# A new order of all steps in a fused attention and feed-forward kernel, with the key-value sums in three groups

## The chip, the cores and the metric

The kernel runs on one core of a Trainium2 chip. A core has five engines, each with its own list of instructions: TensorE (PE; its weight loads are listed as PEld), VectorE (DVE), ScalarE (ACT), GpSimd (POOL) and SyncE (SP), which here only issues transfers. Engines wait for each other by semaphores. Matrix products land in PSUM, eight banks, which this kernel uses as four pairs. The metric is the device time of one execution in microseconds (us); the median of several runs counts.

## The reference

For 2048 tokens of width 448 the result is `x + A(xn) + B(xn)` with `xn` the layer norm of `x`. A is linear attention with 16 heads of 28, B a feed-forward block of width 1792:

```
q, k, v = split(xn @ wqkv)
pq, pk  = q @ w_phi, k @ w_phi                      # per head
phi     = concat(softmax(p), softmax(-p))           # for q and for k
kv, z   = sum_s phi_k[s]^T v[s],  sum_s phi_k[s]
A       = ((phi_q @ kv) / (phi_q . z + 1e-6)) @ wo
h       = xn @ w1 + b1
B       = (h * tanh(softplus(h))) @ w2              # Mish
```

## The kernel before

All inputs are loaded once and stay on chip. The 2048 tokens are 16 tiles of 128 (t), or 8 pairs of tiles (u). Every step of the program has a short name, and one string, `ORDER`, lists 341 of these names. The steps are called in that order, each step appends its operations to the lists of the engines that it uses (`Program.op`, line 53), and what an operation reads and writes gives its waits. So `ORDER` fixes the order on every engine at once, and also which pair of PSUM banks a product gets (`take2`, line 380: the pair unused the longest), hence whose eviction it waits for. A step that comes later on an engine never overtakes an earlier one that waits.

The names, by stage:

- Loads on SP's queue: `lx..s` (x), `lkms`, `lvms`, `lkts` (key and value weights), `lqT0`..`3` (query weights, transposed), `l1ms` and `l1ts` (W1, main part and last rows), `l2s` (W2), `los` (Wo).
- Layer norm of pair u: `st` (statistics on DVE, `bn` and an aggregate for each tile; `b`: one of the two tiles on ACT), `rs` (reciprocal deviation, on POOL or ACT), `xn` (normalise, `d` on DVE, `p` on POOL, which needs a small `shift` from DVE first), `xt` (transposed copy xT: `a`, `b` by PE and an eviction, `m` by a DMA transpose on SP's queue).
- Weights: `wtk`, `wmk`, `wmq` fold w_phi into the key and query weights (Wpk, Wpq); `qd` copies a few columns of WqT on DVE before `wmq`; `pw` and `bd` prepare the block-diagonal w_phi on POOL.
- Products of pair u: `k`, `q`, `v`. Each has 14 matmuls of 64 rows ("passes") in three parts, A (6), B (6) and H (2), which `ORDER` places one by one; the part that comes last brings the eviction. That is two exponentials on ACT for k (`exk`, to the tile E) and for q (`exq`, to Eq), one copy for v (its engine is the letter of the last part, `a` ACT or `d` DVE).
- `kn{u}.{s}` (lines 623 to 631): half of pair u's key features is summed and inverted on DVE, then scaled on POOL (L630). `kv{u}` (L649): 32 small matmuls that add pair u to the key-value sums, all in one PSUM pair. `kvz` (line 656): DVE evicts the sums into KVT, SP's queue transposes KVT to KVZ.
- `e{t}`: DMA transpose of tile t's query exponentials to EqT. Eq has three homes (u mod 3), so `exq` of pair u waits for the transposes of pair u - 3.
- `f{q}.{fc}` + A, B or H: first feed-forward product, half q of the tokens, chunk fc of 14; 14 passes of 512 columns; the last part brings the Mish on ACT (L699). Exp and Mish lie in different tables of ACT, so each change between them loads a table.
- `nd{t}` (L722): numerator and denominator of tile t, 16 small matmuls, then seven operations on DVE (L738 to L749), the last of which writes the tile `o`. Two buffers hold `o`, for even and for odd pairs. `ot{u}m`: DMA transpose of o (pair u).
- `wo{u}` + part (L845) and `g{t}` (L828): output product and second feed-forward product, added in one bank for each tile; when all four parts are there, `fin` on DVE (L793) adds x. `sto`, `stt`: stores.
- `zero`, `pi`, `pm`, `pp`, `pv`, `pk`: constants written by POOL: zeros for the warm-up products `z12`, the identity, a mask, padding columns of Eq, ones beside v, and `pk` the zeroing of KVT.

Before the change the eight sums stand in a row in `ORDER` but for one `kn` and some `e` (which PE does not see): `kv3 kn6.0 kv0 e0 kv5 kv1 kn6.1 kv2 kv4 e10 e11 kv7 ep kv6 kvz`. Line 423 is the helper `run` that issues all passes of k, q, v and f; line 512 and 510 the evictions on DVE and ACT.

Of the kernel before, what the change touches and what calls it, by code (L numbers as in the profile page):

```python
# [38 lines left out]
class Program:  # L39
# [13 lines left out]
    def op(self, eng, fn, r=(), w=(), dma=False, tag="", after=()):  # L53
        o = Op()
        o.tag, o.parts = tag, None
        o.eng, o.fn, o.dma, o.needed, o.count, o.sem = eng, fn, dma, False, 0, None
        o.idx = len(self.ops[eng])
        deps = list(after)
        for res in list(r) + list(w):
            if res[0] == "ps":  # L60
                deps += [a for e, a in self.psum.get(res, {}).items() if e != eng]
        for res in r:
            if res[0] != "ps":
                deps += self.writers.get(res, [])
        for res in w:
            if res[0] != "ps":
                deps += [d for d in self.writers.get(res, []) if d.dma or dma or d.eng != eng]
                deps += [d for d in self.readers.get(res, []) if d.dma or dma or d.eng != eng]
        for res in r:
            if res[0] == "ps":  # L70
                self.psum.setdefault(res, {})[eng] = o
            else:
                self.readers.setdefault(res, []).append(o)
        for res in w:
            if res[0] == "ps":
                self.psum.setdefault(res, {})[eng] = o
            else:
                self.writers[res] = [o]
                self.readers[res] = []
        o.deps = deps  # L80
        self.ops[eng].append(o)
        self.order = getattr(self, "order", [])
        self.order.append(o)
        return o

    def dma(self, eng, fn, r=(), w=(), tag=""):
        return self.op(eng, fn, r, w, dma=True, tag=tag)
# [57 lines left out]


ORDER = """
table pw lx2s lba zero lx3s lkms pp lps st2b st3b pi pm rs2p lkts z12 rs3a lx1s b1 bd xn2d wtk0b xn3d xt2b lvms wtk1b
lx4s wmk0b st1 lqT2 xt3a v2Ad wmk1a v2Ha lqT0 st4 rs1a v3Ba k2H v2Bd lqT1 lqT3 rs4p qd lx0s xn1d k2A lx6s v3Ha v3Aa
wmq0d wmq1a xn4d k2B k3A k3H xt1m q3B k3B st5 xt4m q3A st0 k1A l1ts pk q1H k1H rs5p q3H q1A k1B v1Hd xn5p rs0p st6  # L150
rs6p st7 xt5m e7 xn0d v1Ad xt0m q1B q2A q2H v1Bd k4B pv xn6d rs7p kn3.1 kn1.1 q2B xn7d k4A k4H e3 v5Bd kn4.0 k5A xt6m
k5H v5Ad k5B v0Ba e6 k0A k0H v0Aa v0Ha k0B kn1.0 v6Bd xt7m l1ms v5Hd q6B v6Ad q6H kn0.1 e4 q6A v7Ba k7B v7Hd v6Ha k7H
k7A k6H kn5.0 k6A v4Bd v7Aa kn2.0 kn0.0 v4Hd e2 l2s v4Ad k6B q4H kn7.1 q4A kn2.1 f1.2B q4B kn5.1 f0.1B f0.0A e9 f0.0H
f0.1A f1.3B f0.1H kn7.0 f1.3H f1.3A f0.0B f0.2B f1.2H e12 f1.2A e13 q7H f0.2A f0.2H q0A q0H f1.1A q0B e5 q7A q5A e8
kn4.1 q5H kn3.0 q7B q5B f1.1H f0.10H f0.10A f1.1B kv3 kn6.0 kv0 e0 kv5 kv1 kn6.1 kv2 kv4 e10 e11 kv7 ep kv6 kvz f1.7B
f0.10B f1.7A f1.7H f1.10A f1.10H f0.3A e1 f1.11H f1.10B f0.3H f1.13H f0.3B f1.11A f1.13B e14 nd2 f1.12B f1.11B f1.13A
f0.9H f1.12A f1.12H nd1 f0.9A f0.8B f0.9B f0.8A nd3 ot1m f0.12A f0.13H f0.8H f0.12B f0.13B f0.12H f1.5B nd6 f1.5A
f1.5H los f0.7A f0.13A f0.11B e15 f1.8B f0.11H nd0 f0.11A f1.8A f1.8H f0.7B f1.0B ot0m f0.7H f0.5A f1.0H f0.5H nd7
f1.0A f0.5B f1.6B f1.4H f1.9H f1.6H f1.9B f1.6A nd5 f1.4A ot3m f1.9A f0.4B f1.4B f0.6B nd4 f0.6A f0.4H f0.6H wo3B
f0.4A nd10 wo1A wo3A wo3H ot2m nd11 g6 g7 g2 wo0H ot5m wo1H nd15 wo0A nd13 wo1B wo0B nd12 g0 g1 g11 ot6m g3 wo5B nd14  # L160
nd8 wo5A wob nd9 ot7m sto3 ot4m wo5H g10 g9 g14 g4 sto0 g8 g5 wo6H wo4H wo2B wo4B wo6B wo7B wo2H wo4A wo2A wo7A wo6A
wo7H g13 sto5 g12 sto6 sto1 sto2 g15 sto4 stt14 stt15
"""


# [5 lines left out]
def _kernel(es, nc, A_x, A_wqkv, A_w_phi, A_wo, B_w1, B_b1, B_w2, out):  # L171
    def sb(name, shape, dtype):
        return es.enter_context(nc.sbuf_tensor(name, shape, dtype))
# [33 lines left out]
    epsT = sb("epsT", [P, 3], FP32)  # L207
# [7 lines left out]
    KVT = sb("KVT", [P, G, 2, 2, 64], BF16)  # L215
# [34 lines left out]
    def bank(b, n=1):  # L250
        return PS[:, b * TCW:(b + n) * TCW]
# [10 lines left out]
    def pb(b):  # L262
        return ("ps", b)
# [82 lines left out]

    def p_kvt():
        op("POOL", lambda e: e.memset(KVT[:, :, :, :, :].rearrange("p g s x f -> p (g s x f)").bitcast(mybir.dt.uint32),
                                      0), w=[("KVT", j) for j in range(4)], tag="pk3")

    def eps_rows():
        for i in range(2):
# [36 lines left out]
    def free2(b):  # L389
        held.discard(b)  # L390
        touch(b, b + 1)
# [264 lines left out]
    def kvz():  # L656
        kvb = kv_bank[0]
        for j in range(4):
            lo, hi = 32 * j, 32 * j + DH + 2
            op("DVE", lambda e, j=j, lo=lo, hi=hi: e.tensor_scalar(  # L660
                KVT[lo:hi, :, :, j // 2, (j % 2) * DH:(j % 2 + 1) * DH],
                bank(kvb)[lo:hi, 0:G * KVW].rearrange("p (g s f) -> p g s f", s=2, f=DH), epsT[lo:hi, 2:3], None,
                op0=ALU.add),
               r=[pb(kvb), ("epsT", 2)], w=[("KVT", j)], tag=f"kvz{j}")
        free2(kvb)
        dma("SP", lambda e: e.dma_start_transpose(KVZ[:, :, :], KVT[:, :, :, :, :].rearrange("p g s x f -> p (g s x f)")),
            r=[("KVT", j) for j in range(4)], w=[("KVZ",)], tag="kvT")
# [231 lines left out]
    for q in range(2):  # L899
        for part in "FABH":  # L900
            for fc in range(FC):
                add(f"f{q}.{fc}{part}", ffn1, q, fc, part)
    add("kvz", kvz)
    add("wob", last_weights)
    add("table", table)
# [16 lines left out]
    for n, fn in (("pi", p_ident), ("pm", p_mask), ("pw", p_wbd), ("pv", p_ones), ("pk", p_kvt), ("pp", p_pads), ("zero", p_zero)):  # L922
        add(n, fn)
# [55 lines left out]
```

## Time and profile before

| what | us |
|---|---|
| median of 3 runs (156.78 to 159.19) | 156.9 |
| the profiled execution: time / its span | 158.34 / 156.0 |
| PE busy | 145.4 |
| DVE busy | 104.2 |
| ACT busy | 74.5 |
| POOL busy | 38.7 |
| last matmul of PE ends at | 152.5 |

In the profile a row of a timeline has the start in us from the span's start, the length, engine, line, operation, what is written from what, and the count; in brackets stand the idle time of the engine before it and what ended that. The chain of waits goes back from the last instruction through what released each. PEclk is the clock that PE was granted, 1.00 being full speed.

### The profile page before, as it was taken

The page shows a single profiled execution, that of the slowest core. Times are in us where ns is not written, and L with a number is a line of the kernel's source. Part 1 is how long each engine was busy: PE and PEld are TensorE (multiplying, and loading weights), DVE is VectorE, ACT ScalarE, POOL GpSimd, SP SyncE. Part 2 cuts the span into 40 slices and gives each one's busy share as a digit, 9 for nine tenths or more (in the row PEclk, how much of TensorE's full clock was granted, in tenths as well). Part 3 has the DMA queues.
Part 4 walks back from the last instruction along what each step waited for, and adds up shares of the span by engine and source line. Part 5 has one row for each costly group of instructions (what it writes and reads, how often), then busy time and mean ns, then how long its engine had stood idle before and what let it go on. Part 6 is the DMA issues. An engine that isn't in the chain of part 4 may idle for free.

```text
span 156.0 us, 3862 instructions
## 1 busy us (share of the span) xinstructions
PE 145.4 (93%) x1669; PEld 75.7 (48%) x1669; DVE 104.2 (67%) x230; ACT 74.5 (48%) x90; POOL 38.7 (25%) x53
## 2 busy tenths in 40 slices
PE   6899998699999984999999999999999999999992
PEld 2365454355544452444443445555555555547451
DVE  1699999999999502209985778993995799003511
ACT  4984999569899894557566567300000000000000
POOL 6403285878999930000000000000000000000000
PEclk9999999999999997899999999999999999999999
DMA  4996659989999938460069531613003040600017
GB/s 131 256 253 195 118 132 177 174 168 305 240 303 215 93 71 133 94 113 4 0 38 256 101 39 25 38 25 59 6 0 59 4 118 0 176 0 4 0 38 256
DMA packets 39964, 17.23 MB, mean 110 GB/s; under 512 B 33932, under 2 KB 39180, under 8 KB 39948
## 3 DMA queue, kind: packets, MB, share of 16 engines
q1 hardware_dynamic: 39776, 16.89, 52.1%
q8 instruction: 13, 0.21, 0.5%
q10 hardware_dynamic: 172, 0.10, 0.2%
q14 instruction: 3, 0.02, 0.1%
HBM read 7.02 MB, written 1.84 MB: 57 GB/s over the span
## 4 chain that ended last, share of the span: by engine, by line
PE 75%; DVE 11%; DMA 6%; issue 3%; POOL 2%; ACT 1%; DVEq 0%; POOLq 0%
PE PS L423 34%; PE PS L828 27%; PE PS L845 7%; DMA xnT<-xn 3%; PE PS L364 3%; DVE xn L497 3%; DMA Wkv<-xn 3%; DVE stats L462 3%; PE PS L722 2%; PE PS L649 2%; DVE v_all L512 1%; POOL xn L492 1%; DVE mv L464 1%; DVE Wpq L512 1%; ACT actT L680 1%
## 5 line engine op out<-in xcount | busy, mean ns | idle before, releaser
L423 PE MATMUL PS<-xnT,W 64*128 64x512 bf16 x392 | 46.2, 383 | 0.3 <-DVE v_all L744 0.3
L828 PE MATMUL PS<-W,actT 128*128 128x448 bf16 (+1 forms) x224 | 42.7, 351 | 0.0
L699 ACT ACTIVATE actT<-PS,b1T 128x1024 bf16<-128x1024 f32 x28 | 30.3, 1113 | 15.0 <-PE PS L423 14.9
L828 PEld LDWEIGHTS PS<-W,actT 128*128 128x128 bf16 x224 | 21.6, 98 | 20.1 <-issue 0.6
L423 PEld LDWEIGHTS PS<-xnT,W 64*128 64x128 bf16 x392 | 18.5, 95 | 22.5 <-issue 2.5
L630 POOL TENSOR_TENSOR actT<-actT,rSk 128x896 bf16<-128x896 bf16 x16 | 26.7, 1701 | 4.1 <-DVE rSk L628 4.1
L793 DVE TENSOR_TENSOR x_all<-PS,x_all 128x448 bf16<-128x448 f32 (+1 forms) x16 | 9.2, 613 | 18.1 <-PE PS L845 10.5
L626 DVE TENSOR_REDUCE Sk<-actT 128x32 f32<-128x896 bf16 x16 | 16.6, 1040 | 0.2 <-ACT actT L618 0.2
L423 PE MATMUL PS<-Wkv,xnT 64*128 64x448 bf16 x112 | 13.2, 349 | 1.9 <-DMA xnT<-xn 1.9
L618 ACT ACTIVATE actT<-PS 128x896 bf16<-128x896 f32 x16 | 13.8, 924 | 1.0 <-DVE rSk L628 0.6
L423 PE MATMUL PS<-Wpk,xnT 64*128 64x448 bf16 x112 | 13.3, 350 | 0.2 <-ACT Wpk L510 0.2
L423 PE MATMUL PS<-Wpq,xnT 64*128 64x448 bf16 x112 | 12.8, 349 | 0.0
L738 DVE COPY Sq<-PS 128x16 f32<-128x16 f32 x32 | 4.0, 167 | 12.0 <-PE PS L722 11.9
L749 DVE TENSOR_TENSOR xn<-v_all,rden 128x448 bf16<-128x448 f32 x16 | 10.0, 625 | 2.4 <-DMA Wkv<-xn 1.8
L462 DVE BATCH_NORM_STATS2 stats<-x_all 128x6 f32<-128x448 bf16 x14 | 8.4, 601 | 3.4 <-DMA x_all<-in_A_x_dram 3.4
L746 DVE TENSOR_TENSOR v_all<-v_all 128x464 f32<-128x464 f32 x16 | 10.3, 642 | 0.6
L742 DVE TENSOR_TENSOR v_all<-PS,Sq 128x464 f32<-128x464 f32 x16 | 10.3, 641 | 0.5
L744 DVE TENSOR_TENSOR v_all<-PS,Sq 128x464 f32<-128x464 f32 x16 | 10.1, 630 | 0.0
L423 PEld LDWEIGHTS PS<-Wkv,xnT 64*128 64x128 bf16 x112 | 5.7, 94 | 6.7 <-issue 2.7
L680 ACT ACTIVATE actT<-PS 128x896 bf16<-128x896 f32 x10 | 8.5, 925 | 0.7 <-PE PS L423 0.7
L497 DVE TENSOR_SCALAR xn<-x_all,mv,rstd 128x448 bf16<-128x448 bf16 (+2 forms) x21 | 8.5, 458 | 0.0
L423 PEld LDWEIGHTS PS<-Wpk,xnT 64*128 64x128 bf16 x112 | 5.7, 94 | 5.4 <-ACT Wpk L510 0.6
(83 smaller groups left out, 117.7 us busy)
## 6 DMA issues: line engine op xcount, KB each, us to landing
W<-in_B_w_dram SPq DMA_DIRECT2D x1, 1568.0 KB, 8.6
out_dram<-x_all SPq DMA_DIRECT2D x7, 224.0 KB, 2.2
W<-in_B_w_dram SPq DMA_DIRECT2D x1, 1344.0 KB, 7.0
x_all<-in_A_x_dram SPq DMA_DIRECT2D x4, 224.0 KB, 3.3
x_all<-in_A_x_dram SPq DMA_DIRECT2D x2, 448.0 KB, 4.8
Wkv<-in_A_wqkv_dram SPq DMA_DIRECT2D x2, 336.0 KB, 4.8
Wo<-in_A_wo_dram SPq DMA_DIRECT2D x2, 336.0 KB, 4.4
W<-in_B_w_dram SPq DMA_DIRECT2D x2, 224.0 KB, 3.7
```

The lines of the kernel that those rows point to most:

```text
L423: ins = e.matmul(o, lhs(c, k), rhs(c, k), start=first and n == at[par][0], stop=last and n == at[par][-1])
L462: op("DVE", lambda e, t=t: e.bn_stats(stats[:, t, :], x_all[:, t, :]), r=[("x", t)], w=[("st", t)], tag=f"bn{t}")
L497: op("DVE", lambda e, t=t, lo=lo, hi=hi, at=at: e.tensor_scalar(X[:, at:at + hi - lo], x_all[:, t, lo:hi], mv[:, t, 0:1], rstd[:, t:t + 1] ...
L618: op("ACT", lambda e, s=s: e.activation(E_of(u)[:, s, :, :], two(b, D), ACT.Exp, scale=1.0 if s == 0 else -1.0), r=[pb(b), pb(b + 1)], w=[ ...
L626: op("DVE", lambda e: e.tensor_reduce(Sk[u][:, s, :], Eh(), AX.X, ALU.add), r=[("E", u, s)], w=[("Sk", u, s)], tag=f"Sk{u}.{s}")
L630: op("POOL", lambda e: e.tensor_tensor(Eh(), Eh(), ap_on(rSk[u][:, s, 0:1], [[1, 2 * H], [0, DH]]), ALU.mult), r=[("E", u, s), ("rSk", u, ...
L699: op("ACT", lambda e: e.activation(actT[:, fc, q * 1024:(q + 1) * 1024], bank(b, 2), ACT.Mish, bias=b1T[:, fc:fc + 1]), r=[("b1T",), pb(b) ...
L742: op("DVE", lambda e: e.tensor_tensor(tv(t1[i]), num(0), sx(1), ALU.mult), r=[pb(b), pb(b + 1), ("Sq", i, 1)], w=[("t1", i)], tag=f"ta{t}")
L744: op("DVE", lambda e: e.tensor_tensor(tv(t2), num(1), sx(0), ALU.mult), r=[pb(b), pb(b + 1), ("Sq", i, 0)], w=[("t2",)], tag=f"tb{t}")
L746: op("DVE", lambda e: e.tensor_tensor(t1[i], t1[i], t2, ALU.add), r=[("t1", i), ("t2",)], w=[("t1", i)], tag=f"tc{t}")
L828: ins = e.matmul(bank(b)[:, 0:width(t)], actT[:, fc, tok(t)], W2[:, fc, 0:width(t)], start=first and fc == 0, stop=last and fc == FC - 1)
L845: ins = e.matmul(bank(b)[:, 0:w], oT_of(u)[lo:hi, cc * P:(cc + 1) * P], Wo[lo:hi, cc, 0:w], start=first and n == at[par][0], stop=last and ...
```

## The change

All 341 steps get a new order. What the products, the evictions and the stores compute is unchanged. Beside the order itself:

- the eight sums stand in three groups, `kv5 kv0 kv2`, then `kv7 kv4 kv6`, then `kv3 kv1`. On PE `q7A q5A f0.13A q5H f0.13B` stand between the first two, `f0.13H f0.6H f0.6A f0.10A f0.6B f0.10B` between the last two;
- the part that ends v2 is `v2Aa`, so ACT evicts it and not DVE;
- `e3 e2` come ahead of `l1ms`; `l2s`, `e15` and `los` come behind `kvz`; `l1ts` ahead of `xt4m`;
- POOL begins with `pv` instead of `pw`, `pw` moves behind `rs2p`, and `pp` moves behind `pk`;
- the zeroing of KVT writes a resource of its own, ("KVT0",), and `kvz` reads it, where the zeroing had written the four resources that `kvz` writes.

```diff
--- before.py
+++ after.py
@@ -145,21 +145,21 @@
 
 
 ORDER = """
-table pw lx2s lba zero lx3s lkms pp lps st2b st3b pi pm rs2p lkts z12 rs3a lx1s b1 bd xn2d wtk0b xn3d xt2b lvms wtk1b
-lx4s wmk0b st1 lqT2 xt3a v2Ad wmk1a v2Ha lqT0 st4 rs1a v3Ba k2H v2Bd lqT1 lqT3 rs4p qd lx0s xn1d k2A lx6s v3Ha v3Aa
-wmq0d wmq1a xn4d k2B k3A k3H xt1m q3B k3B st5 xt4m q3A st0 k1A l1ts pk q1H k1H rs5p q3H q1A k1B v1Hd xn5p rs0p st6
-rs6p st7 xt5m e7 xn0d v1Ad xt0m q1B q2A q2H v1Bd k4B pv xn6d rs7p kn3.1 kn1.1 q2B xn7d k4A k4H e3 v5Bd kn4.0 k5A xt6m
-k5H v5Ad k5B v0Ba e6 k0A k0H v0Aa v0Ha k0B kn1.0 v6Bd xt7m l1ms v5Hd q6B v6Ad q6H kn0.1 e4 q6A v7Ba k7B v7Hd v6Ha k7H
-k7A k6H kn5.0 k6A v4Bd v7Aa kn2.0 kn0.0 v4Hd e2 l2s v4Ad k6B q4H kn7.1 q4A kn2.1 f1.2B q4B kn5.1 f0.1B f0.0A e9 f0.0H
-f0.1A f1.3B f0.1H kn7.0 f1.3H f1.3A f0.0B f0.2B f1.2H e12 f1.2A e13 q7H f0.2A f0.2H q0A q0H f1.1A q0B e5 q7A q5A e8
-kn4.1 q5H kn3.0 q7B q5B f1.1H f0.10H f0.10A f1.1B kv3 kn6.0 kv0 e0 kv5 kv1 kn6.1 kv2 kv4 e10 e11 kv7 ep kv6 kvz f1.7B
-f0.10B f1.7A f1.7H f1.10A f1.10H f0.3A e1 f1.11H f1.10B f0.3H f1.13H f0.3B f1.11A f1.13B e14 nd2 f1.12B f1.11B f1.13A
-f0.9H f1.12A f1.12H nd1 f0.9A f0.8B f0.9B f0.8A nd3 ot1m f0.12A f0.13H f0.8H f0.12B f0.13B f0.12H f1.5B nd6 f1.5A
-f1.5H los f0.7A f0.13A f0.11B e15 f1.8B f0.11H nd0 f0.11A f1.8A f1.8H f0.7B f1.0B ot0m f0.7H f0.5A f1.0H f0.5H nd7
-f1.0A f0.5B f1.6B f1.4H f1.9H f1.6H f1.9B f1.6A nd5 f1.4A ot3m f1.9A f0.4B f1.4B f0.6B nd4 f0.6A f0.4H f0.6H wo3B
-f0.4A nd10 wo1A wo3A wo3H ot2m nd11 g6 g7 g2 wo0H ot5m wo1H nd15 wo0A nd13 wo1B wo0B nd12 g0 g1 g11 ot6m g3 wo5B nd14
-nd8 wo5A wob nd9 ot7m sto3 ot4m wo5H g10 g9 g14 g4 sto0 g8 g5 wo6H wo4H wo2B wo4B wo6B wo7B wo2H wo4A wo2A wo7A wo6A
-wo7H g13 sto5 g12 sto6 sto1 sto2 g15 sto4 stt14 stt15
+pv table lx2s lba zero pm st2b lx3s lkms lps st3b lkts z12 pi b1 rs2p pw rs3a xn2d bd lx1s wtk0b lvms lx4s xn3d xt2b
+wtk1b wmk0b lqT2 xt3a v2Ha wmk1a v2Ba lqT0 st1 v3Ha lqT1 lqT3 rs1a v3Aa v2Aa st4 rs4p pk v3Ba k3H lx0s k3A qd xn1d
+wmq0d wmq1a k2H k3B lx6s pp k2A st5 q3A xn4d k2B q3B rs5p q2A xt1m l1ts q3H k1A q2H xn5p xt4m st0 v1Ad k1H st6 xt5m e7
+rs0p q2B st7 xn0d v1Bd k1B v1Hd rs7p rs6p k4A k4H q1B k4B xn6d q1H q1A v4Ad k5H xn7d v4Hd k5A v4Bd v5Ad kn1.0 xt0m k5B
+v5Bd k0B xt6m v5Hd xt7m v0Ba kn2.1 kn2.0 k0H k0A e3 k6H k6A kn0.0 e2 v6Ba l1ms k6B v0Ha kn0.1 v0Aa v6Aa v6Ha k7H k7A
+q4B e6 k7B v7Aa v7Ha kn7.0 q4H q4A q6A q6H v7Ba e9 q6B kn6.0 f0.2B kn5.1 f0.0A f1.2A f0.2A f0.0H f1.2H kn6.1 e5 f1.3B
+f0.2H f0.0B e12 f1.2B f1.3A kn4.1 f0.3B kn5.0 f1.3H e13 f0.3H f0.1B e4 f0.3A f0.1H f0.1A q7H q0A kn3.1 q0H kn4.0 q5B
+e8 q0B q7B kv5 kn7.1 e0 kv0 kv2 q7A q5A f0.13A q5H f0.13B kv7 kv4 e10 kv6 f0.13H f0.6H f0.6A kn3.0 f0.10A f0.6B kn1.1
+f0.10B kv3 kv1 ep f0.10H f1.7H f1.7A e11 f1.9A kvz f1.7B f0.12B f1.5B f0.12A f1.5H f0.5H f1.9H f0.12H l2s f1.9B f1.5A
+f0.5A f1.1A nd3 f1.1B f0.5B e15 f1.0A f1.1H f1.13B f1.0H f1.13H f1.0B nd2 los f1.13A ot1m f1.8B f0.9H f1.8A f1.8H nd0
+f0.11B f0.9A f0.11A f0.11H f0.7A f0.7H f0.8B nd6 e14 f0.8H f0.9B f0.7B e1 f0.8A f1.12H f1.12A f1.10A nd7 f1.10B f1.4H
+f1.10H f1.12B ot3m f1.4A nd1 f1.6B f1.4B f0.4H f1.6A ot0m f0.4A wo1H f1.6H f0.4B nd4 wo1A wo3A wo1B wo3H nd5 ot2m g1
+g3 g2 f1.11A f1.11H nd11 wo0B f1.11B wo3B wo0A nd13 wo0H nd10 g6 ot5m g0 g7 g11 nd12 wo2A wo5A sto1 ot6m wo5H wo2B
+nd15 nd9 g10 sto0 g5 nd14 ot7m wo2H wo5B nd8 g4 g9 g14 g13 g12 g8 sto3 ot4m wo4H wo4A wo6B wo7B sto2 wo6H wo6A sto5
+wo4B sto4 wo7H wob wo7A g15 stt14 sto6 stt15
 """
 
 
@@ -346,7 +346,7 @@
 
     def p_kvt():
         op("POOL", lambda e: e.memset(KVT[:, :, :, :, :].rearrange("p g s x f -> p (g s x f)").bitcast(mybir.dt.uint32),
-                                      0), w=[("KVT", j) for j in range(4)], tag="pk3")
+                                      0), w=[("KVT0",)], tag="pk3")
 
     def eps_rows():
         for i in range(2):
@@ -661,7 +661,7 @@
                 KVT[lo:hi, :, :, j // 2, (j % 2) * DH:(j % 2 + 1) * DH],
                 bank(kvb)[lo:hi, 0:G * KVW].rearrange("p (g s f) -> p g s f", s=2, f=DH), epsT[lo:hi, 2:3], None,
                 op0=ALU.add),
-               r=[pb(kvb), ("epsT", 2)], w=[("KVT", j)], tag=f"kvz{j}")
+               r=[pb(kvb), ("epsT", 2), ("KVT0",)], w=[("KVT", j)], tag=f"kvz{j}")
         free2(kvb)
         dma("SP", lambda e: e.dma_start_transpose(KVZ[:, :, :], KVT[:, :, :, :, :].rearrange("p g s x f -> p (g s x f)")),
             r=[("KVT", j) for j in range(4)], w=[("KVZ",)], tag="kvT")
```

## The prediction

> **What bounds the kernel now.** I read the page first: share of the engines, the slices, the chain that ended last.
>
> ```profile
> span 156.0 us, 3862 instructions
> PE 145.4 (93%) x1669; PEld 75.7 (48%) x1669; DVE 104.2 (67%) x230; ACT 74.5 (48%) x90; POOL 38.7 (25%) x53
> PEclk9999999999999997899999999999999999999999
> q8 instruction: 13, 0.21, 0.5%
> PE 75%; DVE 11%; DMA 6%; issue 3%; POOL 2%; ACT 1%; DVEq 0%; POOLq 0%
> ```
>
> TensorE (PE) bounds it. The order moves work about but drops no product, so it can win only what PE loses: its gaps, and the time at a low clock. So next I read PE's timeline for every gap behind the start. A matmul's row ends about 0.26 us after the next may start, so I measure a gap from start to start, with the spacing of passes (one 64-row matmul of a product) from stretches without a gap.
>
> ```profile
> 10.70 0.93 PE L423 MATMUL PS<-Wkv,xnT 64*128 64x448 bf16 x8
> 11.84 0.36 PE L423 MATMUL PS<-Wpk,xnT 64*128 64x448 bf16 x2 [0.21 <-ACT Wpk L510]
> ...
> 13.17 0.92 PE L423 MATMUL PS<-Wkv,xnT 64*128 64x448 bf16 x8
> 14.16 0.96 PE L580 MATMUL PS<-Wbd,WqT 112*128 112x112 bf16 x16
> ...
> 24.26 0.92 PE L423 MATMUL PS<-Wpk,xnT 64*128 64x448 bf16 x8
> 25.64 0.74 PE L423 MATMUL PS<-Wkv,xnT 64*128 64x448 bf16 x6 [0.46 <-DMA xnT<-xn]
> ...
> 27.52 0.75 PE L423 MATMUL PS<-Wpk,xnT 64*128 64x448 bf16 x6
> 29.72 0.74 PE L423 MATMUL PS<-Wkv,xnT 64*128 64x448 bf16 x6 [1.45 <-DMA xnT<-xn]
> 30.29 0.94 PE L423 MATMUL PS<-Wpk,xnT 64*128 64x448 bf16 x8
> 31.04 0.75 PE L423 MATMUL PS<-Wkv,xnT 64*128 64x448 bf16 x6
> ...
> 42.47 6.24 PE L423 MATMUL PS<-xnT,W 64*128 64x512 bf16 x56
> 48.55 0.35 PE L423 MATMUL PS<-Wpq,xnT 64*128 64x448 bf16 x2
> ...
> 54.04 1.89 PE L423 MATMUL PS<-xnT,W 64*128 64x512 bf16 x16
> 56.23 2.01 PE L649 MATMUL PS<-actT,v_all 128*30 128x56 bf16 x223 [0.30 <-ACT actT L680]
> 60.85 0.58 PE L649 MATMUL PS<-actT,v_all 128*30 128x56 bf16 x33 [2.62 <-issue]
> ...
> 83.11 2.32 PE L423 MATMUL PS<-xnT,W 64*128 64x512 bf16 x20
> 85.77 2.12 PE L423 MATMUL PS<-xnT,W 64*128 64x512 bf16 x18 [0.33 <-DVE v_all L744]
> ```
>
> Eight passes of 448 columns take 31.04 - 30.29, 0.094 us each; 56 of 512 take 48.55 - 42.47, 0.109 each. The gaps are then: 11.84 - 10.70 - 8 x 0.094 = 0.39; 14.16 - 13.17 - 0.75 = 0.24; 25.64 - 24.26 - 0.75 = 0.63; 29.72 - 27.52 - 0.56 = 1.64; 56.23 - 54.04 - 16 x 0.109 = 0.45; 85.77 - 83.11 - 20 x 0.109 = 0.48. The largest stands in the key-value sums (L649). The windows show it, and what follows it:
>
> ```profile
> 56.20:58.05 1.85, 1.82 (x223) 1.82 (x224) 0.00 (x0) 1.83 (x3) 0.00 (x0) 1.00 0.20 37
> 58.05:60.85 2.80, 0.18 (x22) 0.08 (x11) 0.00 (x0) 2.16 (x2) 0.00 (x0) 0.91 0.65 94
> 60.85:63.74 2.89, 2.89 (x45) 1.32 (x46) 1.79 (x4) 0.00 (x0) 0.00 (x0) 0.50 0.51 96
> 63.74:66.65 2.91, 2.91 (x30) 1.28 (x28) 0.00 (x0) 2.12 (x2) 0.00 (x0) 1.00 0.74 143
> ```
>
> Columns: stretch, its length, busy time of PE, PEld, DVE, ACT, POOL, then PE's clock. 224 weight loads go in 1.85 us, then 2.80 us of nothing, then 2.89 us at half clock, which loses 2.89 x 0.5 = 1.45. Every loss together: 0.63 at the start (two gaps) + 0.63 + 1.64 + 0.45 + 2.80 + 1.45 + 0.48 = 8.1 us.
>
> **What the 2.80 us wait for.** The view names no releaser ("issue"). The last of the eight sums, kv6, needs POOL's last normalisation; that had ended 2 us earlier. What does fall there is a fetch of instructions, the only one in its window:
>
> ```profile
> 36.14 19.92 POOL L630 TENSOR_TENSOR actT<-actT,rSk 128x896 bf16<-128x896 bf16 x12 [0.56 <-DVE rSk L628]
> q8 instruction: 1, 0.02, 5.8%
> ```
>
> POOL's row ends at 56.06. The second row is the window 57.9 to 59.4. The page counts 13 such fetches for 2 x 1669 weight loads and matmuls, one for some 257; PE eats the sums' 512 in about two microseconds, two fetches' worth. I read the gap as PE out of instructions: its 449th of the stretch could start only 60.85 - 56.23 = 4.62 us after the first. (The Trainium skill, Runtime: NRT & Kernel Launch, Instruction fetch mechanics, gives blocks of 256 instructions, with which 257 agrees, but room for 2048 on PE and fetches mostly hidden. By that the gap is no fetch and splitting the sums wins nothing there: first rival below.)
>
> **The change, part by part.**
>
> *Sums in three groups* (kv5 kv0 kv2, kv7 kv4 kv6, kv3 kv1). A sum takes 1.85/7 = 0.26 us. Between the groups stand 14 passes of q7 and q5 with 12 of f0.13: 14 x 0.094 + 12 x 0.109 = 2.62 us; then 28 ffn1 passes, 3.05. Now 448 instructions from the first sum on last 0.79 + 2.62 + 0.79 + 6 passes, 0.65 = 4.85, against the 4.62 that supply needed: no gap. The sums also start 22 passes earlier in PE's list (q7A, q5A, q5H and 8 of f0.10 no longer precede them), so the fetch falls elsewhere; then PE meets the same limit at 448 + 44 = 492 instructions, after 0.79 + 2.62 + 0.79 + 3.05 = 7.25 us. I take 2.80 as gone; at worst 4.62 - 4.20 = 0.4 of it stays, with the limit right behind the second group. Without a gap over 2 us I see no cause for half clock: 1.45 gone. (The Trainium skill, TensorE: Matmul & The Clock Gate, Part 1, lets the clock fall after an idle window of about 3.4 us. The gap was 2.80 and the clock fell; by the rule as stated the 1.45 would not be tied to this gap, and the sum would be 1.45 higher.)
>
> *v2's eviction goes from DVE to ACT.*
>
> ```profile
> 12.91 1.06 DVE L512 CAST v_all<-PS 128x896 bf16<-128x896 f32 x1
> 13.89 0.21 DVE L286 COPY WqT<-WqT 128x256 bf16<-128x256 bf16 x1
> 16.08 3.37 ACT L618 ACTIVATE actT<-PS 128x896 bf16<-128x896 f32 x4
> ```
>
> The copy in WqT (qd) stood behind it, and PE's L580 at 14.16 behind qd (0.24). Without it qd ends near 13.1. The k passes that waited for Wpk (0.39) now stand behind all of v3. So both go: 0.63. ACT takes the 1.06 in time it waited for v3.
>
> *xT5, xT0, xT6, xT7.* DVE runs about 0.9 us ahead from there.
>
> ```profile
> 24.54 5.04 DMA xnT<-xn
> xnT<-xn SPq DMA_TRANSPOSE x6, 3.3
> ```
>
> xT5 is sent earlier (its shift no longer stands behind bn0 and bn1 on DVE) and its user k5H comes behind k4, q1 and v4A: 0.63 gone. xT0 left at 24.54 and took 5.04, against a median 3.3. It leaves 0.9 to 1.6 earlier, so lands between 26.2 and 28.7. k0B, now its first user, stands 12 passes further down than v0B did: 29.72 - 2.90 (gaps gone) + 12 x 0.094 = 27.95. I let 0.5 of the 1.64 stay (bounds 0 and 0.75).
>
> *W1 behind e3 and e2.* e3 waits for q1's exponentials, now the seventh pair on ACT: from 16.08 - 0.63, 14 x 0.84 (row above) gives 27.2; two issues of 1.31 more, and the load leaves at 30.
>
> ```profile
> W<-in_B_w_dram SPq DMA_DIRECT2D x1, 1344.0 KB, 7.0
> 25.90 1.31 SPq L688 DMA_TRANSPOSE EqT<-actT  x1
> ```
>
> It lands near 37. The first ffn1 pass stands 84 ffn1 and 28 q passes ahead of the sums; these start at 56.23 - 3.35 (gaps) - 22 x 0.094 = 50.8, so it stands at 39.0. Covered by 2 us; beyond that each microsecond costs one. W2, Wo and e15 go behind the sums' transpose; W2's first user g1 comes after 90, 25 us later: nothing.
>
> *POOL and DVE before the sums.* First normalisation after v4's eviction (v4B ends 18 passes ahead of k0B, 26.3; + 1.06 + 1.33 = 28.7); 16 x 19.92/12 = 26.6 gives 55.3. kv1 stands at 50.8 + 7.5 = 58.3, kv7 (needs the 14th, 51.9) at 55.0. Covered by 2 to 3.
>
> ```profile
> 46.54 1.03 DVE L626 TENSOR_REDUCE Sk<-actT 128x32 f32<-128x896 bf16 x1
> 47.87 1.03 DVE L626 TENSOR_REDUCE Sk<-actT 128x32 f32<-128x896 bf16 x1
> ```
>
> *Second half.* The 0.48 at 85.77 comes from DVE, which waited 1.84 us to write o until the transpose of its buffer's former content had landed:
>
> ```profile
> 73.13 0.26 DVE L738 COPY Sq<-PS 128x16 f32<-128x16 f32 x2
> ...
> 76.15 0.25 DVE L738 COPY Sq<-PS 128x16 f32<-128x16 f32 x2
> ...
> 83.69 0.63 DVE L749 TENSOR_TENSOR xn<-v_all,rden 128x448 bf16<-128x448 f32 x1 [1.84 <-DMA Wkv<-xn]
> ```
>
> An nd takes DVE 76.15 - 73.13 = 3.0 us; its write of o comes last. Now nd0, of the other buffer, stands between nd2 and nd6, so 3.0 + 2.5 us lie between the send and the write, against 3.3 for a transpose: gone. nd4 right behind nd1 may wait 0.8 so, but no PE step follows close. On PE, nd3, nd2, nd0, nd6, nd7 stand 36, 22, 34 and 34 passes apart (3.9, 2.4, 3.7, 3.7 us), a pace that DVE can follow.
>
> *The KVT tie and the other POOL steps: nothing.* kvz waited for the memset before too; it ends 45 us ahead of its use, and behind kvz nothing new queues. pv takes pw's place ahead of zero at like size; pw hides in POOL's wait for rs2p and Wraw; pp is done before the first q exponential at about 19.
>
> *Hand-offs grown tight.* Counting through the new list, about ten steps have under 0.5 us to spare (f1.3B on q6's exponentials, f0.10A on q5's, wo3A on ot3, nd11 on fin2). I take 0.8 for all, bounds 0 and 2.
>
> Sum: 8.1 - 0.5 - 0.8 = 6.8 us off the profiled span, 156.0 to 149.2. That execution took 158.3 in all, 2.3 around its span; the median of the runs shown is 156.9, and 156.9 - 6.8 = **150.1**.
>
> **Rivals.**
> 1. The gap is not supply (POOL later than its row says, or any cause that follows the sums): 2.80 and 1.45 stay, 150.1 + 4.25 = 154.4. For: no releaser is named, and it stopped exactly at kv6. Against: POOL's row, the fetch. 0.09.
> 2. The early transposes and W1 come no sooner: 0.63, the rest of 1.64 and 1.5 for W1 come back, 150.1 + 3.3 = 153.4. For: xT0's 5.04 shows how such a transfer can stretch. Against: margins above. 0.12.
> 3. Slower: splitting makes PE run dry twice, at both block ends inside the sums. Two gaps of 2.80 with 1.45 each, 150.1 + 8.5 = 158.6. It decides if supply takes over 7.2 us and not 4.62. 0.04; another 0.05 for tight hand-offs adding up to over 10 us, past 160.
>
> **Numbers.** Forecast 0.70, from 148.8 (all 8.1) to 152. With rival 2 the range is 148.8 to 153.4. Two per cent, about what these runs (156.8 to 159.2) can tell, is 3.1: under 153.8 lie the forecast and rival 2, less a little, 0.81; within, rivals 1 and 3, 0.14; slower 0.05.
>
> **What would show it.** Right: no "issue" idle of PE in the sums, clock 1.00 throughout, sums from about 51 to 59, PE busy without a gap over 0.7 to about 145. Wrong: a gap between the groups; PE waiting on xnT, W or POOL's L630 between 25 and 58; DVE's o rows waiting on a transpose while PE's wo steps wait on them.

## The result and the profile after

| | before | after |
|---|---|---|
| median, us (runs) | 158.05 (156.78 to 159.19, 4) | 151.06 (150.73 to 151.37, 4) |
| profiled execution: time / span | 158.34 / 156.0 | 150.73 / 148.7 |
| PE busy | 145.4 | 144.0 |

The ratio is 0.963, with a 95% interval of 0.959 to 0.968: the change takes 3.7% off. The prediction said 150.1 us, and 149.2 for the span.

The median of before depends on which executions it catches. In the 47 further executions of before that ran beside the experiments, 24 show a mean clock of about 0.989 (158.6 us and a span of 156.2 in the mean), and 23 a clock of about 1.00 (157.0 and 154.7). All executions of after show 0.997 to 1.00.

The page of after, from top to chain:

```profile
span 148.7 us, 3864 instructions
PE 144.0 (97%) x1669; PEld 74.2 (50%) x1669; DVE 102.7 (69%) x229; ACT 74.7 (50%) x91; POOL 38.9 (26%) x53
PEclk9999999999999999999999999999999999999999
PE 92%; DMA 3%; DVE 2%; SPq 1%; issue 0%
```

PE's share of the chain went from 75% to 92%, "issue" from 3% to 0%, and the dip in PEclk is gone. The windows over the three groups of sums of after; columns as in the prediction (stretch, length, busy time of PE, PEld, DVE, ACT, POOL, PE's clock, DMA share and rate):

```profile
50.82:51.70 0.88, 0.88 (x99) 0.84 (x98) 0.81 (x5) 0.87 (x3) 0.88 (x2) 1.00 0.00 0
51.70:54.47 2.77, 2.77 (x34) 1.10 (x27) 1.59 (x1) 2.77 (x5) 2.77 (x2) 1.00 0.63 51
54.47:55.35 0.88, 0.88 (x98) 0.84 (x97) 0.00 (x0) 0.88 (x2) 0.88 (x2) 1.00 0.53 11
55.35:58.48 3.13, 3.13 (x39) 1.28 (x30) 0.00 (x0) 3.10 (x4) 1.32 (x2) 1.00 0.66 127
58.48:59.11 0.63, 0.63 (x66) 0.59 (x64) 0.00 (x0) 0.63 (x1) 0.00 (x0) 1.00 2.07 212
```

In every row PE is busy for the whole length, at clock 1.00. PE's waits over the whole span of after are two, both before 7 us:

```profile
PE PS L364 <- POOL mask L327: 1.4, 1, 1.4
PE PS L556 <- DMA Wkv<-in_A_wqkv_dram: 0.4, 1, 0.4
```

How much PE gained is read from its last group of matmuls (L810), in before and in after:

```profile
152.43 0.57 PE L810 MATMUL PS<-W,actT 128*128 128x64 bf16 x14
```

```profile
145.34 0.57 PE L810 MATMUL PS<-W,actT 128*128 128x64 bf16 x14
```

That is 7.09 us of the 7.3 by which the spans differ; the other 0.2 lies in what follows PE.

### The profile page after: what moved, and what is told of

Its sections match the earlier page's. It is cut to its first block, busy times and chain, and to the rows that moved or that the text cites. A ratio compares the mean times of both kernels' runs of the same rounds, so it can differ in the third digit from the quotient of the medians.

```text
span 148.7 us, 3864 instructions
## 1 busy us (share of the span) xinstructions
PE 144.0 (97%) x1669; PEld 74.2 (50%) x1669; DVE 102.7 (69%) x229; ACT 74.7 (50%) x91; POOL 38.9 (26%) x53
## 4 chain that ended last, share of the span: by engine, by line
PE 92%; DMA 3%; DVE 2%; SPq 1%; issue 0%
PE PS L423 50%; PE PS L828 29%; PE PS L845 7%; DMA Wkv<-in_A_wqkv_dram 3%; PE PS L722 3%; PE PS L649 2%; PE PS L580 1%; DVE xn L497 1%; SPq L270 1%; PE PS L556 0%; PE PS L505 0%; DVE x_all L793 0%; DVE Eq L512 0%; DVE x_all L814 0%
## 5 line engine op out<-in xcount | busy, mean ns | idle before, releaser
L423 PE MATMUL PS<-xnT,W 64*128 64x512 bf16 x392 | 44.8, 377 | 0.0
L699 ACT ACTIVATE actT<-PS,b1T 128x1024 bf16<-128x1024 f32 x28 | 29.8, 1112 | 22.1 <-PE PS L423 22.1
L423 PEld LDWEIGHTS PS<-xnT,W 64*128 64x128 bf16 x392 | 17.9, 94 | 21.9 <-PE PS L423 1.9
L423 PEld LDWEIGHTS PS<-Wpq,xnT 64*128 64x128 bf16 x112 | 5.4, 94 | 5.0 <-ACT actT L680 0.2
```

The lines of the kernel that those rows point to most:

```text
L423: ins = e.matmul(o, lhs(c, k), rhs(c, k), start=first and n == at[par][0], stop=last and n == at[par][-1])
L699: op("ACT", lambda e: e.activation(actT[:, fc, q * 1024:(q + 1) * 1024], bank(b, 2), ACT.Mish, bias=b1T[:, fc:fc + 1]), r=[("b1T",), pb(b) ...
```

## The experiments

The first two experiments start from the kernel before, all others from the kernel after, and every edit moves steps in `ORDER` alone; what is computed stays the same. The theory is the prediction's: PE runs out of instructions in the row of sums, and the other gaps go by earlier work on DVE and SP. The rivals are that the stop has another cause, which the order takes away by the way, and that other parts of the new order carry the gain. A diff shows only the stretch of `ORDER` that moves; what stands before and behind it on the line is left out.

| run | median us (executions) | ratio to before, 95% | spans |
|---|---|---|---|
| sums split in before | 156.68 (10) | 0.995, 0.990 to 0.999 | 153.8 to 155.0 |
| the same, first nd later | 156.28 (10) | 0.994, 0.990 to 0.997 | 153.6 to 154.3 |
| sums in one row in after | 155.02 (4) | 0.985, 0.976 to 0.995 | 152.2 to 153.8 |
| row 12 passes later | 154.84 (1) | | 152.8 |
| row without transposes | 156.03 (1) | | 154.0 |
| after again | 151.18 (6) | 0.958, 0.952 to 0.963 | 148.7 to 149.4 |
| W2 early | 152.27 (6) | 0.965, 0.957 to 0.972 | 149.8 to 152.1 |
| v2 on DVE | 152.57 (4) | 0.966, 0.959 to 0.973 | 149.5 to 150.7 |
| xn5 later | 151.72 (1) | | 149.7 |
| b1 later | 151.21 (6) | 0.958, 0.953 to 0.963 | 148.6 to 149.0 |
| lkms second | 151.28 (6) | 0.957, 0.952 to 0.963 | 148.9 to 149.3 |
| both of these | 151.33 (6) | 0.958, 0.954 to 0.963 | 148.8 to 149.1 |

**1. The split alone, in before.** The eight sums become three groups, with passes from right behind them put between:

```diff
-f1.1B kv3 kn6.0 kv0 e0 kv5 kv1 kn6.1 kv2 kv4 e10 e11 kv7 ep kv6 kvz f1.7B
-f0.10B f1.7A f1.7H f1.10A f1.10H f0.3A
+f1.1B kn6.0 kn6.1 kv4 kv3 kv0 e0 f0.10B f1.7B f1.7A kv5 kv1 kv2 e10 e11
+f1.7H f1.10A f1.10H kv7 ep kv6 kvz f0.3A
```

> The order of before with one thing changed: the eight sums in three groups, kv4 kv3 kv0, then 18 ffn1 passes, kv5 kv1 kv2, then 10 ffn1 passes, kv7 kv6. Supply theory (PE runs out of instructions when 448 of them go in under 2 us): no idle over 0.3 us in the sums, clock 1.00 all along, span 156.0 - 2.80 - 1.45 = 151.8 (151.3 to 152.4). Rival (the gap is a wait of the sum kv6 for POOL or another producer): a gap of 2 to 3 us stays in front of kv6's group and the span stays within 1 us of before.

The gap is gone, and the mean clock stayed at 0.997 to 1.00 in all ten executions. Yet the span expected, 151.3 to 152.4, was missed: the spans have a mean of 154.4, only about 0.3 us under those of before without the low clock (154.7). PE's timeline of the split kernel around the sums:

```profile
57.23 0.95 PE L649 MATMUL PS<-actT,v_all 128*30 128x56 bf16 x96 [0.85 <-ACT actT L680]
...
63.29 4.37 PE L423 MATMUL PS<-xnT,W 64*128 64x512 bf16 x36
68.69 0.40 PE L722 MATMUL PS<-KVZ,EqT 56*128 56x60 bf16 x16 [1.03 <-DMA KVZ<-KVT]
```

PE's waits of before list no KVZ at all; here PE waits 1.03 us for it, and 0.85 for ACT ahead of the sums. The wait for KVZ comes of my edit: it took 28 passes from behind the sums, so 36 are left to cover DVE's eviction and the transpose, which need 68.69 - 63.29 = 5.4 us. In before the stretch from the sums' end to nd2 held 64 passes, part of them at half clock, so the slow clock was cover:

```profile
61.36 8.26 PE L423 MATMUL PS<-xnT,W 64*128 64x512 bf16 x64
```

So the 2.80 us of the gap are not all to be had by removing it alone. How much of them other lateness ate (the 0.85 for ACT stands ahead of the sums, where before waited 0.30, and no gap covered that) was not followed to the end.

**2. The first nd later, in the split kernel.** nd2 goes behind two more ffn1 parts:

```diff
-f1.13B e14 nd2 f1.12B f1.11B f1.13A
+f1.13B e14 f1.12B f1.11B nd2 f1.13A
```

> split_in_before with one thing more: 12 ffn1 passes moved from behind the first nd step to ahead of it, so that PE has 1.3 us more work while the sums are evicted and transposed. Theory: the 2.8 us that the split freed came back as waits behind it, 1.3 of them at that nd step, since 28 of the passes that had covered the transpose were used up between the groups. With the cover back, PE's wait for KVZ is under 0.3 and the span 1.0 to 1.3 below split_in_before's (153.8 to 155.0), so 152.6 to 153.9. Rival: the split's gain is lost elsewhere and the span stays.

The wait for KVZ is gone; spans are about 0.4 us shorter than in experiment 1, not the 1.0 to 1.3 expected. Two waits on ACT stand in the view of PE's waits:

```profile
PE PS L649 <- ACT actT L680: 0.5, 1, 0.5
PE PS L423 <- ACT actT L699: 0.4, 1, 0.4
```

The exponentials of k and q, and the Mish behind them, are in time only in the new order. The split in before's order thus gives back the half clock and at most a microsecond more (spans of 154.0 in the mean, against 154.7).

**3. One row again, in after.** The passes between the groups go ahead of the sums:

```diff
-q7B kv5 kn7.1 e0 kv0 kv2 q7A q5A f0.13A q5H f0.13B kv7 kv4 e10 kv6 f0.13H f0.6H f0.6A kn3.0 f0.10A f0.6B kn1.1
-f0.10B kv3 kv1 ep f0.10H f1.7H
+q7B kn7.1 e0 q7A q5A f0.13A q5H f0.13B kn3.0 kn1.1 e10 f0.6A f0.6B kv5 kv0 kv2 kv7 kv4 kv6 kv3 kv1 ep f0.13H
+f0.6H f0.10A f0.10B f0.10H f1.7H
```

> The order of after with one thing undone: the eight sums in one row, kv5 first and kv1 last, in the place between the products that had stood between them. Supply theory: PE stops at the same place of its instruction list as in the kernel before, its 727th weight load; the row begins behind 519, so after 208 loads of the row, inside the seventh sum. Gap 2.5 to 3 us, then about 3 us at half clock; span 148.7 + 4.3 = 153.0 (152.2 to 153.8). Rival (a wait of one sum for its producer): a stop in front of a sum, after 192 or 224 loads, or none.

The gap comes back, in the sums but not at the same sum: here PE stops inside the seventh, where before it stopped at the eighth.

```profile
56.00 2.01 PE L649 MATMUL PS<-actT,v_all 128*30 128x56 bf16 x207
60.06 0.56 PE L649 MATMUL PS<-actT,v_all 128*30 128x56 bf16 x49 [2.05 <-issue]
```

Two executions kept the clock (spans 152.2 and 152.3), two have 0.987 to 0.989 (153.6 and 153.8). Against after's 149.1 the row costs 3.2 us without the low clock and 4.6 with it. Of the 3.2, 2.4 is the row's longer stay (60.55 - 56.00 = 4.55, against 2.1 for eight sums). It also starts 1.2 later than after's first sum and the 38 passes now ahead of it make (50.82 + 14 x 0.094 + 24 x 0.109 = 54.75). Half of that, 0.6, is there from the start (PE's first product passes stand at 10.16, in after at 9.56); most of the rest lies in two gaps of under 0.4 ahead of the row, which were not followed.

**4. The row 12 passes later.** As 3, with `f0.10A f0.10B` ahead of the row too. If the stop hangs on a step or a transfer, it stays at that sum; if it hangs on the number of instructions, it comes 12 matmuls of the sums earlier.

```diff
-e10 f0.6A f0.6B kv5 kv0
+e10 f0.6A f0.6B f0.10A f0.10B kv5 kv0
```

> As row_in_after, with 12 more ffn1 passes ahead of the row. Supply theory: the stop comes 12 loads earlier in the row, after 196 of its loads, again the 727th of the list, with the same gap of 2.5 to 3 us. Rival: the stop stays in front of the same sum as in row_in_after, or goes, since its producers have 1.3 us more.

```profile
57.05 2.08 PE L649 MATMUL PS<-actT,v_all 128*30 128x56 bf16 x195
61.07 0.66 PE L649 MATMUL PS<-actT,v_all 128*30 128x56 bf16 x61 [1.93 <-issue]
```

It moved by 207 - 195 = 12 matmuls. So the stop hangs on no step and no transfer. The windows from zero to a point in the gap count every matmul (first x) and weight load (second x) up to the stop, in before, in 3 and in 4:

```profile
0.00:58.06 58.06, 53.41 (x726) 28.55 (x727) 46.58 (x97) 48.41 (x67) 38.48 (x52) 1.00 0.89 190
```

```profile
0.00:57.90 57.90, 55.62 (x726) 29.74 (x726) 45.27 (x96) 50.99 (x69) 38.58 (x52) 1.00 0.75 163
```

```profile
0.00:59.05 59.05, 56.65 (x726) 30.12 (x726) 45.05 (x96) 51.02 (x69) 38.48 (x52) 1.00 0.75 165
```

Three orders, three points among the sums and three times, and each stops behind the 726th matmul of PE's list. (Experiment 5 does too: x726 up to 58.50.) No semaphore, bank or transfer of the program is common to these places; the count of instructions is.

**5. The row with no transpose beside it.** As 3, with `e10` and `e11` behind `kvz`, to see whether transfers on SP's queue lengthen the gap.

```diff
-kn1.1 e10 f0.6A
+kn1.1 f0.6A
...
-f1.7A e11 f1.9A kvz f1.7B
+f1.7A f1.9A kvz e10 e11 f1.7B
```

> As row_in_after, with the two query transposes e10 and e11 behind the sums' own transpose, so that no transpose is in flight when PE's instructions are fetched. If the fetch is slowed by transposes beside it (its packet took 1.40 us in before against 0.93 in the median), the gap is 0.4 to 1 us shorter than in row_in_after, 1.8 to 2.4 us, and may leave the clock at 1.00. If the gap is the fetch's own latency, it stays within 0.2 us.

The gap, and the DMA view of the window 56 to 60.2 in 40 slices of 0.105 us:

```profile
55.98 1.87 PE L649 MATMUL PS<-actT,v_all 128*30 128x56 bf16 x207
60.19 0.56 PE L649 MATMUL PS<-actT,v_all 128*30 128x56 bf16 x49 [2.35 <-issue]
```

```profile
DMA  0000000000000070000000000000000000000000
q8 instruction: 1, 0.02, 2.0%
```

One instruction fetch, from about 57.5, is all that moves; the gap is 2.35 against 2.05 with transposes. So it isn't contention that makes it long. PE stops at 57.85, after the fetch began, and goes on 2.6 us behind its start. Half of that is the packet itself: 2.0% of 16 engines over 4.2 us are 1.3 us (in before 1.4, with a median of 0.97 over its 13 fetches). What passes in the other 1.3 us the trace doesn't show. Then the clock fell, as it does in about half of before's executions:

```profile
61.09:64.50 3.41, 3.28 (x16) 0.73 (x14) 1.53 (x4) 2.12 (x2) 0.00 (x0) 0.50 0.21 42
```

**6. W2 early.** The load of W2 goes back ahead of the query transposes, the prediction's "nothing":

```diff
-v7Ha v7Ba e9 q6B
+v7Ha v7Ba l2s e9 q6B
...
-f0.12H l2s f1.9B
+f0.12H f1.9B
```

> The order of after with one thing undone: the load of W2 stands ahead of e9 again, as in the kernel before, and not behind the sums' transpose. The prediction put the move at nothing: span within 0.3 of after. Rival: the 1.6 MB lie in front of the query transposes e9 to e8, which land some 6 us later, the exponentials q0 and q7 wait for their home and PE for their banks: 1 to 3 us more.

The median span is 150.25 against 149.1, and the profiled one is 2.2 longer: the expectation's rival came true. PE's timeline, ACT's, SP's, and the DMA issues at 33.5, all of W2 early:

```profile
55.44 0.82 PE L423 MATMUL PS<-xnT,W 64*128 64x512 bf16 x6 [2.46 <-ACT Eq L680]
```

```profile
52.36 1.28 ACT L680 ACT_TABLE_LOAD   x1 [2.86 <-DMA EqT<-Eq]
```

```profile
33.52 1.03 SPq L300 DMA_DIRECT2D W<-in_B_w_dram  x1
39.13 6.34 SPq L688 DMA_TRANSPOSE EqT<-actT  x2
45.51 2.69 SPq L688 DMA_TRANSPOSE EqT<-Eq  x2
48.24 3.80 SPq L688 DMA_TRANSPOSE EqT<-actT  x2
```

```profile
W<-in_B_w_dram SPq DMA_DIRECT2D x1, 1568.0 KB, 12.2
```

W2 takes 12.2 us here (7.9 in after), with W1, sent at 31.61, still in flight beside it until about 38.4, and the last of the transposes is sent by 52.0. In after, SP's timeline has them out by 47.3:

```profile
41.80 2.71 SPq L688 DMA_TRANSPOSE EqT<-Eq  x2
44.56 2.71 SPq L688 DMA_TRANSPOSE EqT<-actT  x2
```

An exponential that reuses a home of Eq, and the table load ahead of it, wait for the transpose, and PE waits for that exponential's bank. The move costs nothing at W2's own user, as predicted; but without it the passes among the sums are late. It is worth 1 to 2 us.

**7. v2 on DVE.** The eviction goes back to DVE:

```diff
-v3Aa v2Aa st4 rs4p
+v3Aa st4 v2Ad rs4p
```

> The order of after with one thing undone: DVE evicts v2, in its place ahead of the copy qd. Theory: qd ends 1.1 us later, PE waits 0.3 to 0.5 for it ahead of L580, and the transposes xT5, xT0, xT6 leave up to 1.0 later, so PE waits another 0.3 to 1 for xnT; span 149.3 to 150.8. Rival: the later work has room, span within 0.2 of after.

The median span is 150.55, 1.45 more. DVE's timeline, and PE's:

```profile
13.26 1.09 DVE L512 CAST v_all<-PS 128x896 bf16<-128x896 f32 x1 [0.18 <-PE PS L423]
14.26 1.22 DVE L286 COPY WqT<-WqT 128x256 bf16<-128x256 bf16 x1
```

```profile
13.62 0.92 PE L423 MATMUL PS<-Wpk,xnT 64*128 64x448 bf16 x8
15.55 0.96 PE L580 MATMUL PS<-Wbd,WqT 112*128 112x112 bf16 x16 [1.01 <-DVE WqT L286]
```

The place is the one the prediction named, the price is not: PE's gap is 15.55 - 13.62 - 0.75 = 1.2 us, five times the 0.24 read in before, and the copy shows 1.22 us instead of 0.21. Why the copy is longer here was not tried. One thing stands beside it: POOL zeroes KVT and writes the padding columns without a break from 14.13 to 15.41, and the copy, begun at 14.26, ends at 15.48; in before it was over by 14.10, when the zeroing of KVT had just begun (14.04), and in after by 13.36, ahead of all these writes. The wait for xnT that was expected too is not listed. This execution also waited 1.1 and 0.8 for the key and value weights, which the edit does not touch.

**8. xn5 later.** DVE's and POOL's work for tile 0 goes ahead of pair 5's normalisation, so that xT5 leaves later:

```diff
-q2H xn5p xt4m st0 v1Ad
+q2H xt4m st0 xn5p v1Ad
```

> The order of after with one thing undone: xn5 stands behind the statistics of pair 0 on DVE again, so xT5 leaves 1.4 us later and, behind it on SP's queue, xT0 about 0.6 later. Theory: xT5 has room (it landed at 23.3, k5 needed it at 25.2), so no wait there; xT0 landed at 28.0 against its need at 28.2, so PE waits 0.2 to 0.7 for xnT. Rival: both have room, no wait.

The view of waits lists none for xnT; the 0.6 us over after's span go with a wait at the start (the key weights, 1.3 us). At k0B, which needs xT0, PE's passes start 0.2 late (29.16, where six passes behind 28.38 would end at 28.95), but the profile of after run again has the same 0.2 there (28.63 for 28.41) without the edit. A miss, as far as one execution shows: xT5 has more room than this edit takes.

**9. Three tries to go below after.** They shorten the start: the statistics that ACT takes for one tile go later (first diff), the key weights are sent second (second diff), and both together.

```diff
-zero pm st2b lx3s lkms lps st3b lkts z12 pi b1 rs2p pw
+zero pm st2b lx3s lkms lps st3b lkts z12 pi rs2p pw
...
-lqT0 st1 v3Ha
+lqT0 st1 b1 v3Ha
```

```diff
-pm st2b lx3s lkms lps
+pm st2b lkms lx3s lps
```

> The order of after with one step moved: b1 (a small transpose on PE behind the warm-up products, and its eviction on DVE) comes behind st1 and no longer stands ahead of the first normalisation xn2 on DVE. Theory: the two levels of the span come from the warm-up, which takes 4.8 us in some executions and 5.3 in others; DVE waits for b1 behind it, and xn2 behind that. With b1 out of the way xn2 starts near 6.25 in all of them; spans 148.5 to 148.8, one level, 0.3 us less in the mean than after. Rival: the levels have another cause, and the same two stay.

> An attempt to beat after: its order with the load of the key weights ahead of the second load of x on SP's queue. PE's first weight transposes wait for it (landed 6.68 in the profile of after, later in others), the x tiles behind it have room. Theory: the weights land 0.4 earlier, and the executions whose start is late get 0.2 to 0.6 better; spans 148.5 to 149.1 against 148.7 to 149.4. Rival: DVE sets the start, no change.

> lkms_second and b1_later together. Theory: with b1 off DVE the key weights' landing sets the start, so both together give 0.3 to 0.5 us: spans 148.2 to 148.7. Rival: the start is set by x's statistics, and nothing is gained over after.

All three lie at 151.2 to 151.3, like after run again (151.18). With b1 later the spans do fall a little, nearly as expected (148.8 in the mean, after 149.05), but the time outside the span grows from 2.0 to 2.4 and takes it back. With the key weights second, PE waits for DVE's first normalisation instead, 0.98 us at 8.35, and with both edits 0.97 at 8.08: the start is held by two paths of like length. No version beat after.

> The kernel after, unchanged, as the measure for the other three on the same chip. Its four executions so far had spans of 148.7 twice and 149.3 twice; the same two levels are expected, time 150.7 to 151.5.

## Why the prediction came out right

PE's timeline of after at the places of the old gaps:

```profile
12.83 0.92 PE L423 MATMUL PS<-Wpk,xnT 64*128 64x448 bf16 x8
13.68 0.96 PE L580 MATMUL PS<-Wbd,WqT 112*128 112x112 bf16 x16
...
28.20 0.73 PE L423 MATMUL PS<-Wpk,xnT 64*128 64x448 bf16 x6
...
38.98 9.25 PE L423 MATMUL PS<-xnT,W 64*128 64x512 bf16 x84
48.07 2.81 PE L423 MATMUL PS<-Wpq,xnT 64*128 64x448 bf16 x28
50.82 0.95 PE L649 MATMUL PS<-actT,v_all 128*30 128x56 bf16 x96
```

- **Up to the sums.** Predicted: 3.35 us of gaps gone, the sums at 50.8. Measured: 50.82, and 56.23 - 50.82 less 22 passes is 3.3. The terms at the start, xT5, xT0 and the bank ahead of the sums all went as booked, together; only v2's and xT5's were tried alone, v2's is larger by itself than its row said, and xT5's cost nothing that could be told apart.
- **xT0.** The transfer leaves at 23.55 and takes 4.5, so it lands at about 28.0, in the predicted 26.2 to 28.7; k0B stands at 28.20 without a wait. The 0.5 that I let stay did not come here, but the margin was 0.2 us, and in the profile of after run again, where the transfer leaves at 23.77 and takes 4.7, 0.2 of it did: a little more, and a part of rival 2 would have come true. The issue, and the DMA issues of its window:

```profile
23.55 1.22 SPq L517 DMA_TRANSPOSE xnT<-xn  x1
```

```profile
xnT<-xn SPq DMA_TRANSPOSE x1, 4.5
```

- **W1.** The load is issued at 31.15, a microsecond later than predicted, and takes 7.0: it lands near 38.2, and its first user stands at 38.98 (predicted 39.0). The cover was 0.8 us, not 2. The page's DMA issues of after, W2 and W1:

```profile
W<-in_B_w_dram SPq DMA_DIRECT2D x1, 1568.0 KB, 7.9
...
W<-in_B_w_dram SPq DMA_DIRECT2D x1, 1344.0 KB, 7.0
```

- **POOL.** The normalisations start at 29.25 and end at 56.6 (predicted 28.7 and 55.3); kv1 follows at 58.8, so they are hidden.

```profile
29.25 1.70 POOL L630 TENSOR_TENSOR actT<-actT,rSk 128x896 bf16<-128x896 bf16 x1 [4.38 <-DVE rSk L628]
31.71 24.88 POOL L630 TENSOR_TENSOR actT<-actT,rSk 128x896 bf16<-128x896 bf16 x15 [0.76 <-DVE rSk L628]
```

- **The sums.** That the stop is bound to a place in PE's list, and to no step or transfer, is shown by experiments 3 to 5; rival 1 falls, and so does rival 3, since no gap stands between the groups. That it is the supply of instructions is the reading that fits the fetches. In the traces' DMA records the fifth of the 13 starts at 57.93, 57.70, 58.56 and 57.57 in before and in experiments 3, 4 and 5, and matmul 727 starts 2.9, 2.4, 2.5 and 2.6 us later, behind the stop. In experiments 1 and 2 and in after that fetch starts at 59.02, 58.48 and 53.56, matmul 727 comes 3.7, 3.7 and 4.6 us later, and there is no stop. So laying other products between the sums gives the fetch its time. (The Trainium skill, Runtime: NRT & Kernel Launch, Instruction fetch mechanics, has room for 2048 instructions on PE, and fetches mostly hidden. The runs differ: with 512 small instructions in a row PE stood for 2.0 to 2.8 us each time.) The groups themselves cost 0.88 + 0.88 + 0.63 = 2.39 us, against 2.1 in a row, which the sum left out. And the 2.80 were to be had only with the rest of the order: experiments 1 and 2 won 0.3 and 0.7 beside the clock.
- **The clock.** The fall goes with the gap: no execution of after or of the split kernels shows it, while with the row it comes in some executions and not in others. (The Trainium skill, TensorE: Matmul & The Clock Gate, Part 1, gives a window of about 3.4 us that runs freely. The 3.41 us at half clock agree with its length.) An idle stretch of 2.35 us was enough for the fall in experiment 5, while one of 2.46 in experiment 6 did not bring it, so the length of the gap alone does not decide. Its place does, as far as the traces go. Their clock records change only at whole multiples of 3.413 us behind the first rise to 1.00: in before that rise is at 5.71, and the half clock lasts from 60.33, which is 5.71 + 16 x 3.413, to 63.74. Here are the windows of this grid that hold most of the idle time, in before, in experiment 5 (first rise at 6.48) and in experiment 6 (5.71):

```profile
56.91:60.33 3.42, 1.32 (x159) 1.22 (x147) 0.00 (x0) 3.28 (x4) 0.00 (x0) 1.00 0.47 61
```

```profile
57.68:61.09 3.41, 1.06 (x73) 0.72 (x62) 0.26 (x1) 0.15 (x1) 0.00 (x0) 1.00 0.00 0
```

```profile
53.50:56.91 3.41, 1.47 (x14) 0.52 (x14) 0.00 (x0) 3.40 (x6) 3.16 (x3) 1.00 0.13 24
```

PE worked 1.32 and 1.06 us in the first two, and the window behind ran at half clock; it worked 1.47 in the third, and 1.76 and 1.92 in those of experiments 3 and 4 (58.47 to 61.88 and 57.21 to 60.62), and the clock stayed. So a gap of the same length may bring the fall or not, by where it lies on the grid. This is a pattern of five traces; no run moved a gap along the grid on purpose, and of the executions without a profile only the mean clock is on record.
- **Second half.** Predicted: no wait, 0.8 for tight hand-offs. No wait is listed. Behind the sums' start after runs 22 passes more (2.2 us) in 145.34 - 50.82 = 94.52 against 152.43 - 56.23 = 96.20, so 3.9 of the expected 4.73 were won; 0.3 of the rest are the groups, and the other 0.5 is spread over hand-offs of under 0.12 us each, which no view lists as a wait.
- **Booked at nothing.** W2's move was, and is worth about 1.15 us in the new order (experiment 6). POOL's moved steps were too, and in after PE waits for POOL no longer than in before (1.4 us at the start); with v2 back on DVE they stand beside the long copy (experiment 7).
- **The sum.** 8.1 in terms, 7.1 on PE, 6.8 predicted. Of the two allowances, 1.3 in all, the 0.5 for xT0 did not come in this execution; 0.5 of the 0.8 for hand-offs did, and the 0.3 of the groups, which the sum had left out, made up for part of the rest. That the total fits so well is luck in part. (A reading to put right, on which nothing rests: in the rows shown, a row ends 0.15 to 0.19 us after the next may start, and not 0.26.)

The step that was off is the last, "156.9 - 6.8": the 6.8 hold 1.45 for the half clock, from an execution of 158.34 us that had it, while 156.9 lies under all 24 executions that have it (157.6 and more). From 158.34 the same terms give 151.5; from 156.9 without the 1.45 they give 151.6. Measured were 151.06. So the gain was 0.5 too small, the start 1.45 too low, and the forecast ended 1.0 under: two errors that partly cancel.

**What stays open:** the tie between the zeroing of KVT and `kvz` was not tried alone; `kvz` shows no wait for POOL. Nor does a trace show what passes between the end of a fetch's packet and PE's next instruction (1.3 us in experiment 5), or which instructions the packet held.

## What to carry to other kernels

Count the instructions of a stretch of small matmuls against the pace at which it runs: here a row of 512 in two microseconds stalled PE, and other products laid between them cost 0.3 us. A gap's length is what it could be worth, not what it is worth: ask what it covers, for here the split alone won 0.3 to 0.7 us beside the clock, and undoing it in the new order lost about three, 2.4 of them in the row itself. Before subtracting a term from a median, see whether the executions behind the median contain that term.

## What the hardware did that I had not expected

- The stop is bound to a place in the list, behind matmul 726 in each of three orders, and PE goes on only 2.4 to 2.9 us behind the start of the fetch, in experiment 5 with no other transfer in flight.
- The same gap brings the low mean clock in about half of before's executions (24 of 47) and not in the others, at 1.6 us apiece. In the traces the half clock comes in whole windows of 3.41 us on a fixed grid, behind a window in which PE worked 1.32 us or less; one with 1.47 did not bring it.
- A transfer ahead in SP's queue delays a whole train of transposes: W2 early, with W1 still in flight, took 12.2 us instead of 7.9, and the last of the transposes behind it was sent 4.7 us later (52.0 against 47.3).
